# Holding the late attention products behind the FFN products in TensorE's order

## The chip, the core and the metric

The kernel runs on one core of a Trainium2 chip. The metric is the device time of one execution in microseconds (us). TensorE (PE) multiplies, VectorE (DVE), ScalarE (ACT) and GpSimd (POOL) do the elementwise work, and SyncE (SP) issues nearly all the transfers. Each engine works through its own queue in order.

## The reference

A windowed attention is followed by an FFN whose activation is a rational function. Of 768 keys a query keeps the first 8 and the 96 up to its own.

```python
scores = scale * np.matmul(q, k.transpose(0, 1, 3, 2)) + bias      # 4 batches, 8 heads, 768 rows, 64 wide
a = softmax(np.where(keep, scores, -1e9))
x = np.matmul(a, v).transpose(0, 2, 1, 3).reshape(3072, 512)
h = x @ w_in                                                       # 512 -> 2048
P = a0 + a1*h + a2*h*h + a3*h*h*h
Q = 1 + |b0|*|h| + |b1|*h*h
out = (P / (Q + 1e-6)) @ w_out                                     # 2048 -> 512
```

## The kernel before

**Units.** The attention is cut into 96 units: a unit u is 128 query rows and two heads. Eight units make a chunk of 256 rows. The FFN is cut into 96 steps f, eight per chunk: step f makes 256 of the 2048 hidden columns for the chunk's 256 rows. So step f of chunk c can begin only when all eight units of the chunk have delivered their rows of x, and chunk c is units 8c to 8c+7 and FFN steps 8c to 8c+7.

**FFN step.** `st_ffn1` (line 280) makes the FFN's first products, 24 of 256 columns into a PSUM tile `h` (two buffers). `st_ew1` to `st_ew4` evaluate the rational function: lines 304 to 306 on ACT, 311 and 312 on DVE, 313 on POOL, 320 and 321 on ACT, 325 to 327 on DVE, 335 on ACT and 336 on POOL, which end in the tile `g`. `st_ffn2` (line 356) makes the second products, 12 of 512 columns into `acc`, two steps after the first products.

**Late attention.** Units from 24 (`PLAIN`) on take a longer way. `st_split` splits k and q into two parts (line 418 ACT, 419 POOL) and sends the q part through two DMAs (lines 422, 423, tile `qT`). `st_score` makes four products (line 442, tile `s`) and the masked result (line 455, DVE); `st_soft` the exponential (line 465, ACT). `st_turn` transposes blocks on DVE (lines 538, 540) and writes them to DRAM (line 542, tile `put`); `st_back` reads them back (line 550, tile `pT`). Every four units `st_pv` makes the products of V and P (line 577, tile `o`; `o24` is units 24 to 27), and `st_x` scales them (line 603, DVE) and stores x as a high and a low part (`xh`, line 608, ACT; `xl`, line 609, DVE).

**What sets the order.** The loop over t in `windowed` emits the steps. Each call of `on` sets a priority for what it emits, from the step's number times 1000 and a table `PRI`. A scheduler then lays out every engine's queue: of what it believes ready it takes the smallest priority. It has no instruction to keep attention and FFN in step with each other. In the loop, f trails t by 10 to 14 steps.

Of the kernel before, what the change touches and what calls it, by code (L numbers as in the profile page):

```python
# [35 lines left out]
PLAIN = 24  # L36
# [73 lines left out]
def tile_kernel(ctx: ExitStack, tc: tile.TileContext, q, k, qk, v, n_global, n_local,  # L110
                w_in, w_out, ca, cb, out):
    nc = tc.nc
# [26 lines left out]
    def st_load(u, other=nc.sync):  # L139
        c, t, p, b, i = unit(u)  # L140
        hs = slice(2 * p, 2 * p + 4)
        r = slice(i * P, (i + 1) * P)
        if u >= PLAIN:
            nat[u // 2] = pl.ldp.tile([P, 2, 2, P], F32, tag="nat", name=f"kq{u}")
            nc.sync.dma_start(out=nat[u // 2], in_=qk[b, i, p // 2])
            return
        n = pl.ldp.tile([P, 2, 4, D], F32, tag="nat", name=f"nat{u}")
        nc.sync.dma_start(out=n[:, 0], in_=q[b, hs, r, :].rearrange("h s d -> s h d"))
        other.dma_start(out=n[:, 1], in_=k[b, hs, r, :].rearrange("h s d -> s h d"))
        nat[u // 2] = n  # L150
# [73 lines left out]
    def pieces(kind, n):  # L224
        if kind:
            return [(1, 2 * (n % 2) + x, n // 2) for x in range(2)]
        return [(0, 2 * n + x) for x in range(2)]
# [60 lines left out]
    def is_last(f):  # L288
        return f == NU - 1 and not pl.split
# [325 lines left out]
    def windowed(lates):  # L615
        first = [key for t in sorted(WSCHED) for kind, j in WSCHED[t] for key in pieces(kind, j)][0:GBUFS + 3]
        scope = ExitStack()
        pl.early = scope.enter_context(tc.tile_pool(name="early", bufs=1))
        pl.rr = const.tile([P, Q], F32, name="rr")
        pl.rT = const.tile([P, Q], F32, name="rT")  # L620
        nc.gpsimd.memset(pl.rr, 1.0)
        pl.kF = pl.early.tile([P, NPAIR, 2, P], F32, name="kF")
        pl.kGF = pl.early.tile([P, NPAIR, G], F32, name="kGF")
        pl.qz = pl.early.tile([P, 3, 2, P], F32, name="qz")
        nc.scalar.dma_start(out=ni[:, 0:2], in_=n_local.bitcast(I32).partition_broadcast(1))
        nc.scalar.dma_start(out=ni[:, 2:4], in_=n_global.bitcast(I32).partition_broadcast(1))
        st_load(0, nc.scalar)
        st_load(2, nc.scalar)
        st_load_v(0)
        st_load_v(2)  # L630
        nc.scalar.preload_act_table_set("natural_log_exp_and_others")
        for n, key in enumerate(first):
            fetch(key)
        make_identity(nc, ident)
        for x in range(2):
            nc.gpsimd.memset(pl.qz[(1 - x) * D:(2 - x) * D, :, x, :], 0.0)
        one = tmp("one")[0:1, 0, 0:P]
        n1 = pl.early.tile([1, 4], F32, name="n1")
        nc.gpsimd.memset(one, 1.0)
        nc.vector.tensor_copy(out=n1, in_=ni)  # L640
        n_ps = pl.ps_r.tile(sh, F32, tag="r", name="n_ps")
        nc.tensor.matmul(out=n_ps[:, 0, 0:4], lhsT=one, rhs=n1, start=True, stop=True)
        nc.vector.tensor_copy(out=nf, in_=n_ps[:, 0, 0:4])
        nl, ng = nf[:, 0:1], nf[:, 2:3]
        scr = tmp("scr").rearrange("p a (b w) -> p (a b) w", w=P)
        scr = [scr[:, x, :] for x in range(4)]
        window_masks(nc, scr, masks[:, 2, 2, :], masks[:, 2], nl, ng)
        load_coef()

        base = tc.cur_priority  # L650

        def scaled_mask(h):
            if 0 <= h < H and h != 2:
                nc.vector.tensor_scalar(out=masks[:, h], in0=masks[:, 2], scalar1=2.0 ** (2 - h), scalar2=None,
                                        op0=ALU.mult)

        def turn(f):
            return f + EARLY_LAG + (LAG - EARLY_LAG) * min(max(f - FPC, 0), 2 * FPC) / (2 * FPC)

        f = -1  # L660
        for t in range(NU + LAG + F2 + 1):
            step = int(turn(f + 1)) <= t
            f += step
            when = {True: 1000 * turn(f), False: 1000 * t}
            pri = {True: PRI_A if f < FPC else PRI, False: PRI_A if t < FPC + EARLY_LAG else PRI}

            def on(name, fn, u, *args, ffn=False, more=0):
                if 0 <= u < NU:
                    tc.cur_priority = int(base + when[ffn] + pri[ffn][name] + more)
                    fn(u, *args)  # L670

            def ffn(name, fn, u, *args):
                if step:
                    on(name, fn, u, *args, ffn=True)

            def pv(u, more):
                on("pv", st_pv, u, more=more)
                on("x", st_x, u, more=more)

            def behind(n):  # L680
                now, past = t - n, t - n - 1
                return [u for u in ((past,) if past >= PLAIN else ()) + ((now,) if now < PLAIN else ())]

            if t % 2 == 0:
                if t + 4 < PLAIN:
                    on("load", st_load, t + 4)
                if t + 2 >= PLAIN:
                    on("load", st_load, t + 2)
                if t + 4 < PLAIN:
                    on("load", st_load_v, t + 4)  # L690
                elif t - 4 >= PLAIN:
                    on("load", st_load_v, t - 4)
            for u in behind(1):
                on("score", st_score, u)
                on("soft", st_soft, u)
                on("sums", st_sums, u)
            if t == PLAIN:
                scope.close()
                pl.late = lates.enter_context(tc.tile_pool(name="late", bufs=1))
                pl.kq = pl.late.tile([P, 2, 2, 3, 2, P], FR, name="kq")  # L700
                pl.kG = pl.late.tile([P, 2, NPAIR, G], FR, name="kG")
            if t == PLAIN:
                for h in range(H):
                    on("load", scaled_mask, h)
            ffn("ffn1a", st_ffn1, f, 0)
            if t < PLAIN:
                on("qkT", st_qkT, t)
            if t % 2 == 0 and t - 4 >= PLAIN:
                on("turn", st_turn, t - 4)
            if t % 2 == 0 and t - 6 >= PLAIN:  # L710
                on("back", st_back, t - 6, more=65)
            if t % 4 == 2 and t - 6 >= PLAIN:
                on("turn", st_put_rows, t - 6)
            if t % 4 == 0 and t - 8 >= PLAIN:
                on("back", st_get_rows, t - 8)
            if t % 4 == 1 and t - 9 >= PLAIN:
                pv(t - 9, 0)
            if t < PLAIN:
                on("qkE", st_qkE, t)
            elif t % 2 == 0:  # L720
                on("qkE", st_split, t)
            if not is_last(f - 1):
                ffn("ew3", st_ew3, f - 1)
            for u in behind(1):
                on("norm", st_norm, u)
            ffn("ffn1b", st_ffn1, f, 1)
            if is_last(f) and step:
                st_ew4(f - 1)
                last_half(f, 0)
                last_half(f, 1)  # L730
            else:
                ffn("ew1", st_ew1, f)
                if not is_last(f - 1):
                    ffn("ew4", st_ew4, f - 1)
                ffn("ew2", st_ew2, f)
            g = f - F2 if f - F2 < NU - HELD else f - F2 - 1 if f - F2 > NU - HELD else NU
            ffn("ffn2a", st_ffn2, g, 0)
            if t - 2 < PLAIN:
                on("pT", st_pT, t - 2)
            ffn("ffn2b", st_ffn2, g, 1)  # L740
            if t % 2 and t - 3 < PLAIN and spread(t - 3):
                on("turn", st_put_rows, t - 3)
                on("back", st_get_rows, t - 3, more=70)
            if t % 2 and t - 3 < PLAIN:
                pv(t - 3, 0 if t < FPC + EARLY_LAG else 700)
            for n, (kind, j) in enumerate(WSCHED.get(t, ())):
                tc.cur_priority = base + 1000 * t + pri[False]["dec"] + 50 * n
                for key in pieces(kind, j):
                    decode(key)
            if step:  # L750
                for n, key in enumerate(list(full)[SPLITS.get(f - 1, 0):SPLITS.get(f, 0)]):
                    tc.cur_priority = int(base + when[True] + pri[True]["wsplit"] + 4 * n)
                    split_w(key)
        tc.cur_priority = base + 1000 * (NU + LAG + F2 + 5)
# [165 lines left out]
```

## Time and profile before

| | us |
|---|---|
| median of 3 runs (lowest, highest) | 736.69 (736.0, 739.11) |
| the profiled execution: its time | 743.32 |
| the profiled execution: its span, first to last instruction | 741.5 |
| TensorE busy in the span | 707.9 (95%) |
| ACT busy | 569.3 (77%) |
| DVE busy | 537.0 (72%) |
| POOL busy | 426.4 (58%) |

TensorE's matmuls are pipelined, so its busy time does not say that it runs at its peak. How far apart matmuls start says that, and where it sits idle says what it waits for.

### The profile page before, as it was taken

Reading aid. Unit: us, or ns where it says so; the run is one execution under the profiler, and the core shown is the slowest. Engines: PE = TensorE matmul, PEld = TensorE weight load, DVE = VectorE, ACT = ScalarE, POOL = GpSimd, SP = SyncE. Lnnn points to the kernel's source line nnn. Section 1 sums busy time; section 2 is a strip of 40 time slices with the busy share of each in tenths; the row PEclk is TensorE's granted clock in tenths of the full one; section 3 lists DMA queues with packets and bytes.
Section 4 is the critical chain, followed back from the end, with each engine's and each line's share of the span. In section 5 each row is a group of like instructions: output and inputs, shape, how many; then the busy total and the mean of one; then the engine's idle time right before and its main releaser. Section 6 shows DMA issues by size and latency. Waiting matters only on the chain.

```text
span 741.5 us, 13943 instructions
## 1 busy us (share of the span) xinstructions
PE 707.9 (95%) x4618; PEld 601.1 (81%) x4618; DVE 537.0 (72%) x1215; ACT 569.3 (77%) x1232; POOL 426.4 (58%) x421
## 2 busy tenths in 40 slices
PE   5899799999799989999999999999999999999996
PEld 4576367788698778899988888888988889988994
DVE  5777996885877767677877776667786777865665
ACT  6898866888788877688888886667888877866664
POOL 4398775578765664457565764444657646444441
PEclk9999899999899999999999999999999999999999
DMA  9886600114677688016667561010246613510001
GB/s 260 265 247 195 187 23 14 59 47 119 195 211 228 193 219 214 22 37 198 181 186 208 153 191 52 1 35 23 72 143 195 189 47 114 169 50 1 30 0 35
DMA packets 96502, 92.73 MB, mean 125 GB/s; under 512 B 47140, under 2 KB 78500, under 8 KB 96420
## 3 DMA queue, kind: packets, MB, share of 16 engines
q1 hardware_dynamic: 95216, 91.22, 42.3%
q8 instruction: 39, 0.64, 0.4%
q10 hardware_dynamic: 1204, 0.52, 0.3%
q14 instruction: 43, 0.35, 0.1%
HBM read 58.59 MB, written 23.68 MB: 111 GB/s over the span
## 4 chain that ended last, share of the span: by engine, by line
PE 83%; DMA 5%; ACT 4%; DVE 3%; POOL 2%; SPq 1%; issue 1%; POOLq 0%; DVEq 0%; ACTq 0%
PE h L280 32%; PE acc L356 31%; PE o L577 6%; PE s L442 4%; PE acc L351 4%; PE h L272 3%; PE s L436 2%; POOL kq L419 1%; DMA put<-tb 1%; DMA pT<-put 1%; DMA r<-in_moe_w_in_dram 1%; PE tp L526 1%; ACT pr L465 1%; DMA r<-in_moe_w_out_dram 1%; DVE pr L455 1%
## 5 line engine op out<-in xcount | busy, mean ns | idle before, releaser
L313 POOL TENSOR_TENSOR fa<-fa,fs 128x512 f32<-128x512 f32 x95 | 122.8, 1293 | 153.0 <-ACT fs L306 142.0
L280 PE MATMUL h<-xh,win_l 128*128 128x256 f32 x704 | 199.1, 283 | 0.0
L356 PE MATMUL acc<-wout_l,g 128*128 128x512 f32 x352 | 139.4, 396 | 0.0
L280 PEld LDWEIGHTS h<-xh,win_l 128*128 128x128 f32 x704 | 133.5, 190 | 2.5
L336 POOL TENSOR_TENSOR g<-fu,g 128x512 fp32r<-128x512 f32 x87 | 112.3, 1291 | 38.3 <-ACT g L335 32.0
L304 ACT ACTIVATE fu<-h,coef 128x512 f32<-128x512 f32 (+1 forms) x97 | 74.7, 771 | 60.5 <-PE h L280 55.8
L325 DVE SCALAR_TENSOR_TENSOR fu<-fu,coef,q 128x512 f32<-128x512 f32 (+1 forms) x97 | 71.5, 737 | 64.6 <-ACT q L321 63.6
L419 POOL TENSOR_TENSOR kq<-kq,kq 64x512 fp32r<-64x512 f32 x72 | 93.3, 1295 | 32.2 <-ACT kq L418 22.1
L465 ACT ACTIVATE pr<-pr,stats 128x256 f32<-128x256 f32 (+1 forms) x192 | 92.6, 485 | 5.5 <-DVE stats L455 4.9
L320 ACT ACTIVATE fs<-fa,coef 128x512 f32<-128x512 f32 (+1 forms) x97 | 69.7, 719 | 34.1 <-POOL fa L313 32.7
L311 DVE TENSOR_TENSOR fu<-fu,h 128x512 f32<-128x512 f32 (+1 forms) x97 | 65.5, 675 | 40.6 <-ACT fs L306 36.5
L356 PEld LDWEIGHTS acc<-wout_l,g 128*128 128x128 f32 x352 | 66.5, 189 | 11.5
L312 DVE SCALAR_TENSOR_TENSOR fu<-fu,coef,h 128x512 f32<-128x512 f32 (+1 forms) x97 | 70.9, 730 | 1.8
L326 DVE SCALAR_TENSOR_TENSOR q<-fa,coef,q 128x512 f32<-128x512 f32 (+1 forms) x97 | 72.1, 743 | 0.0
L306 ACT ACTIVATE fs<-h,coef 128x512 f32<-128x512 f32 (+1 forms) x97 | 65.9, 679 | 3.5 <-DMA out_dram<-o 1.6
L305 ACT ACTIVATE fa<-h,coef 128x512 f32<-128x512 f32 (+1 forms) x97 | 65.4, 675 | 3.3 <-DVE q L326 3.2
L327 DVE SCALAR_TENSOR_TENSOR fu<-q,fu 128x512 f32<-128x512 f32 (+1 forms) x97 | 65.9, 679 | 1.4
L577 PE MATMUL o<-pT,vt 128*64 128x128 f32 x704 | 59.9, 286 | 6.6 <-DMA pT<-put 5.5
L577 PEld LDWEIGHTS o<-pT,vt 128*64 128x64 f32 x704 | 41.3, 138 | 23.7 <-issue 15.6
L538 DVE STREAM_TRANSPOSE tb<-pr 128x512 f32<-128x512 f32 x60 | 42.0, 704 | 24.8 <-DMA put<-tb 21.0
L321 ACT ACTIVATE q<-fs 128x512 f32<-128x512 f32 (+1 forms) x97 | 57.8, 596 | 1.7
L335 ACT CAST g<-fu 128x512 fp32r<-128x512 f32 (+1 forms) x89 | 54.7, 615 | 5.6 <-DVE fu L327 5.2
(260 smaller groups left out, 1895.8 us busy)
## 6 DMA issues: line engine op xcount, KB each, us to landing
put<-tb SPq DMA_DIRECT2D x30, 512.0 KB
pT<-put SPq DMA_DIRECT2D x120, 128.0 KB
kq<-in_qk_dram SPq DMA_DIRECT2D x36, 256.0 KB
qT<-kq SPq DMA_DIRECT2D x72, 128.0 KB
r<-in_moe_w_in_dram SPq DMA_DIRECT2D x16, 512.0 KB
r<-in_moe_w_out_dram SPq DMA_DIRECT2D x16, 512.0 KB
vt<-in_v_dram SPq DMA_DIRECT2D x48, 128.0 KB
out_dram<-o SPq DMA_DIRECT2D x23, 256.0 KB
```

Of the source, the lines that this page charges most:

```text
L280: nc.tensor.matmul(out=hps[f][:, y, :], lhsT=w[:, fs], rhs=x[:, ct, :], start=(n == 0), stop=(n == 3 * NCT - 1))
L304: nc.scalar.activation(out=u, in_=h, func=AF.Identity, scale=a3, bias=a2)
L312: nc.vector.scalar_tensor_tensor(out=u, in0=u, scalar=a1, in1=h, op0=ALU.add, op1=ALU.mult)
L313: side(f).tensor_tensor(out=a, in0=a, in1=s, op=ALU.add)
L320: nc.scalar.activation(out=s, in_=a, func=AF.Ln, bias=q1)
L325: nc.vector.scalar_tensor_tensor(out=u, in0=u, scalar=a0, in1=r, op0=ALU.add, op1=ALU.mult)
L326: nc.vector.scalar_tensor_tensor(out=r, in0=a, scalar=q1, in1=r, op0=ALU.add, op1=ALU.mult)
L336: side(f).tensor_tensor(out=g[:, 1, ys], in0=u, in1=g[:, 0, ys], op=ALU.subtract)
L356: nc.tensor.matmul(out=acc, lhsT=gs[f][:, z, y, ts], rhs=w, start=(ft == 0 and n == 0), stop=(ft == NFT - 1 and n == 2))
L419: nc.gpsimd.tensor_tensor(out=at[other], in0=raw[own], in1=at[own], op=ALU.subtract)
L465: nc.scalar.activation(out=d, in_=d, func=AF.Exp, scale=-1.0, bias=st[:, x:x + 1], accum_out=st[:, 2 + 2 * x:3 + 2 * x])
L577: nc.tensor.matmul(out=o_ps[x * D:(x + 1) * D, y, :], lhsT=vt[:, 2 * (y % 2) + x, :], rhs=turned_p(u0 + y, x, w), start=(n == 0), stop=(n ...
```

## The change

For each loop step t the change notes in `ended[t]` the last TensorE instruction of the FFN's first products (`ffn1b`). From unit 24 on the first score product of a unit gets an order dependency on `ended[t - 1]`, and the first product of a V and P run one on `ended[t]`. Both sides are on TensorE, so that no semaphore and no instruction is added: the dependency binds the scheduler alone.

```diff
         base = tc.cur_priority
+        here = nc.cur_bb.bb
+        ended = {}
+
+        def products(n):
+            return [x for x in list(here.instructions)[n:] if x.engine == mybir.EngineType.PE]
+
+        def behind_ffn(t, n):
+            own = products(n)
+            if own and t in ended:
+                tc.add_manual_dep(own[0], ended[t].name, mybir.DependencyInfo(
+                    mybir.DependencyClass.NoSync, mybir.DependencyReason.DATA), reason="order of late steps")
...
             def pv(u, more):
+                n = len(here.instructions)
                 on("pv", st_pv, u, more=more)
+                if u >= PLAIN:
+                    behind_ffn(t, n)
                 on("x", st_x, u, more=more)
...
             for u in behind(1):
+                n = len(here.instructions)
                 on("score", st_score, u)
+                if u >= PLAIN:
+                    behind_ffn(t - 1, n)
                 on("soft", st_soft, u)
...
+            n = len(here.instructions)
             ffn("ffn1b", st_ffn1, f, 1)
+            ended[t] = (products(n) or [ended.get(t - 1)])[-1]
+            if ended[t] is None:
+                del ended[t]
```

**TensorE's queue where the late units begin.** The number behind `s`, `h` and `o` is the unit, the FFN step and the first unit of a run; `g13` is the g of FFN step 13. Before:

```order
L442 MATMUL s26_2008<-kq_1743 128x256
...
L280 MATMUL h16_2018<-xh2_1380,w1_0_0h_1114 128x256
...
L442 MATMUL s27_2085<-kq_1743 128x256
...
L442 MATMUL s28_2163<-kq_1743 128x256
L280 MATMUL h16_2018<-xl2_1381,w1_2_0h_1036 128x256
...
L442 MATMUL s29_2253<-kq_1743 128x256
...
L442 MATMUL s30_2323<-kq_1743 128x256
L356 MATMUL acc1_0_1458<-w0_10h_1828,g13_1871 128x512
...
L442 MATMUL s31_2354<-kq_1743 128x256
L442 MATMUL s30_2323<-kq_1743,qT30_2206 128x256
...
L577 MATMUL o24_2381<-pT24_2192,vt24_2006 64x128 x4
```

The same place in the queue of the change:

```order
L442 MATMUL s26_2008<-kq_1743 128x256
...
L280 MATMUL h16_2018<-xh2_1380,w1_0_0h_1114 128x256
...
L442 MATMUL s27_2085<-kq_1743 128x256
...
L356 MATMUL acc1_0_1458<-w0_10h_1828,g13_1871 128x512
...
L280 MATMUL h17_2098<-xh2_1380,w1_0_0h_1114 128x256
...
L442 MATMUL s28_2163<-kq_1743 128x256
...
L280 MATMUL h18_2174<-xh2_1380,w1_0_1h_1196 128x256
...
L442 MATMUL s29_2253<-kq_1743 128x256
...
L280 MATMUL h19_2264<-xh2_1380,w1_0_1h_1196 128x256
...
L442 MATMUL s30_2323<-kq_1743 128x256
```

Six units' scores stood within one FFN step, with the first products of V and P right behind; now one unit stands behind each FFN step, and all 24 first products of step 16 stand together.

**TensorE's queue where a chunk's last run of V and P ends.** `o36` is the last run of the chunk whose FFN begins with `h32`. In the change:

```order
L577 MATMUL o36_3342<-pT36_3101,vt36_2886 64x128
...
L280 MATMUL h31_3329<-xh3_2390,w1_0_3h_1718 128x256
...
L356 MATMUL acc3_0_2961<-w0_10h_1828,g29_3297 128x512
...
L442 MATMUL s44_3410<-kq_1743 128x256
...
L356 MATMUL acc3_0_2961<-w0_10h_1828,g29_3297 128x512
...
L280 MATMUL h32_3420<-xh4_3021,w1_0_0h_1114 128x256
```

Before, the same run ended eight FFN steps earlier:

```order
L577 MATMUL o36_3342<-pT36_3101,vt32_2597 64x128
...
L442 MATMUL s44_3410<-kq_1743 128x256
...
L442 MATMUL s45_3497<-kq_1743 128x256
...
L280 MATMUL h24_2735<-xh3_2390,w1_0_0h_1114 128x256
```

The run o36 moved from ahead of FFN step 24 to ahead of the last half of step 31, one step ahead of the one that needs it.

**DVE's queue at that place.** In the change:

```order
L326 SCALAR_TENSOR_TENSOR q30_3364<-fa30_3289,coef_63,q30_3364 128x512
L603 TENSOR_TENSOR o36_3342<-o36_3342,wbyf_2344 128x512
L327 SCALAR_TENSOR_TENSOR fu30_3288<-q30_3364,fu30_3288 128x512
L455 ISA pr44_3415,stats_64<-s44_3410,masks_66 128x256
...
L609 TENSOR_TENSOR xl4_3022<-o36_3342,xh4_3021 128x4x128
```

Two operations of other work now stand between the scaling of o36 and the low part of x, and the scaling stands behind the function's steps of FFN step 30.

## Rows read from the trace of the kernel before

**Rows 1.** Stretches: length; busy PE, PEld, DVE, ACT, POOL; clock, DMA share, GB/s
```profile
150.00:200.00 50.00, 45.53 (x318) 39.56 (x318) 36.41 (x98) 42.25 (x99) 39.60 (x39) 0.99 0.39 107
200.00:250.00 50.00, 48.54 (x344) 42.56 (x341) 38.82 (x101) 41.96 (x96) 30.52 (x36) 0.94 0.75 217
250.00:300.00 50.00, 46.68 (x335) 39.85 (x334) 34.64 (x88) 36.92 (x84) 28.60 (x26) 1.00 0.78 209
350.00:400.00 50.00, 50.00 (x380) 44.84 (x379) 37.99 (x93) 43.02 (x96) 31.48 (x34) 1.00 0.65 192
```
**Rows 2.** Waits of TensorE from 165 us on; us in total, times, longest us
```profile
PE o L577 <- DMA pT<-put: 5.5, 2, 2.8
PE s L442 <- DMA qT<-kq: 1.5, 2, 1.0
PE h L280 <- DVE fu L312: 1.0, 1, 1.0
PE acc L356 <- POOL g L336: 0.6, 1, 0.6
```
**Rows 3.** TensorE in time, first long wait: start, us, instruction, [idle <-releaser]
```profile
180.27 0.28 PE L442 MATMUL s<-kq 128*128 128x256 f32 x1
...
181.22 0.39 PE L280 MATMUL h<-xl,w_0h 128*128 128x256 f32 x1 [0.19 <-DVE xl L609]
...
196.55 0.28 PE L442 MATMUL s<-kq 128*128 128x256 f32 x1
199.48 1.12 PE L577 MATMUL o<-pT,vt 128*64 128x128 f32 x8 [2.65 <-DMA pT<-put]
...
202.40 0.63 PE L356 MATMUL acc<-wout_l,g 128*128 128x512 f32 x1
202.83 0.63 PE L356 MATMUL acc<-w_14h,g 128*128 128x512 f32 x1
```
**Rows 4.** The chain that ended last, near that wait; start us, us, what
```profile
187.85 3.07 DMA put<-tb
...
195.96 3.38 DMA pT<-put
```
**Rows 5.** Stretches of 5 us, columns as in rows 1
```profile
200.00:205.00 5.00, 5.00 (x23) 4.28 (x20) 4.13 (x14) 3.14 (x6) 2.85 (x5) 0.50 0.88 265
...
270.00:275.00 5.00, 3.32 (x22) 2.55 (x23) 2.14 (x5) 4.00 (x13) 4.06 (x4) 1.00 0.94 245
```
**Rows 6.** TensorE in order of time, around a piece of a V and P run
```profile
158.83 0.39 PE L356 MATMUL acc<-w_5h,g 128*128 128x512 f32 x1
159.15 0.66 PE L577 MATMUL o<-pT,vt 128*64 128x128 f32 x8
159.74 0.38 PE L280 MATMUL h<-xh,w_2h 128*128 128x256 f32 x1
159.96 0.28 PE L280 MATMUL h<-xl,w_2h 128*128 128x256 f32 x1
```
**Rows 7.** The chain that ended last: long pieces of V and P, and the last chunk's start
```profile
355.99 1.90 PE o L577 x32
...
678.03 1.46 PE o L577 x24
679.49 1.62 PE h L280 x12
681.11 2.79 PE acc L356 x12
683.89 2.84 PE h L280 x24
```
**Rows 8.** Lines 603, 608, 609: ns min/median/max, first and last start us
```profile
L603 DVE TENSOR_TENSOR o<-o,wbyf x18: 667/698/700, 200.6 to 679.5; 128x512 f32<-128x512 f32 x18
L608 ACT CAST xh<-o x26: 357/585/615, 56.5 to 680.3; 128x512 fp32r<-128x512 f32 x18, 128x256 fp32r<-128x256 f32 x8
L609 DVE TENSOR_TENSOR xl<-o,xh x26: 409/683/692, 56.9 to 680.9; 128x512 fp32r<-128x512 f32 x18, 128x256 fp32r<-128x256 f32 x8
```

## The prediction

> **What bounds the kernel now.** I read the busy time by stretches first. From 350 to 400 us TensorE is busy for all of 50.00 us at full clock; from 150 to 300 us it is not: 45.53, 48.54 and 46.68 us of 50, with a mean clock of 0.94 in the middle stretch [rows 1]. Busy TensorE here means one that starts a matmul as soon as it can. 24 first products of 256 columns take 2.84 us, 0.12 each; 12 second products of 512 columns 2.79 us, 0.23 each [rows 7]. So where TensorE is full, time goes by the count of matmuls, which the change leaves as it is. What can be won is idle time, lost clock, and what it costs to switch between kinds of matmul.
>
> The list of waits says who makes TensorE idle after 165 us: the read-back of the turned P (5.5 us in two waits), qT (1.5), a first product that waits for DVE to free its PSUM buffer (1.0) and a g that is late on POOL (0.6), 8.6 us in all [rows 2]. The matmuls in order of time show how the first of them arises. The score of unit 27 starts at 180.27. Its P is transposed, written out (187.85, 3.07 us) and read back (195.96, 3.38 us) [rows 4], and the run of V and P over units 24 to 27 goes on at 199.48, after 2.65 us of idleness [rows 3]. That way takes 19.2 us. In TensorE's order of before only some 13 us of work stand between that score and that part of the run; scores of units 28 to 33 are among it, which nothing needs yet. TensorE is in order, so the late read-back also holds the FFN products behind it, and they were ready. The chain through the DMAs is the limit of this stage, because the attention was pulled ahead of the FFN work that could have covered it.
>
> **The change, part by part.** It removes and adds no instruction. From unit 24 on it puts one unit's scores behind each FFN step and the runs of V and P one FFN step ahead of where they are needed.
>
> *The waits.* From the score of unit 27 to the run o24 the new order has 72 first products, 16 score products and 48 second products: 88 x 0.12 + 48 x 0.23 = 21.6 us, against the 19.2 us that the data took. That 19.2 us was measured with DVE and POOL crowded by six units at once, so I expect the data earlier. For the other 17 runs the same count gives 20 to 31 us from the last score to the run; before it was 14 us at the second run. Splitting q and k moves too, on ACT, POOL and SP. In the new order each split stands two FFN steps ahead of its score, some 10 us ahead of need once the 3 to 4 us of its transfer are taken off. SP's queue has the write, the four read-backs, two qT transfers and two loads for each pair of units as before, now at an even pace. I therefore take all 8.6 us out. Bounds: 0 if every wait comes back elsewhere, 8.6 if none does; I take the upper one, because from 350 to 400 us the same transfers run at a DMA share of 0.65 without idling TensorE [rows 1].
>
> *The clock.* Behind the 2.65 us wait the clock is at its lower level, 1.2 GHz (0.50), for the whole stretch from 200 to 205 us [rows 5], and second products follow one another by 0.43 us [rows 3] instead of 0.23. At 0.43 instead of 0.23, 5 us of work could have been done in 2.7: 2.3 us that go with the wait. Bounds 0 to 2.3; I take 2.3. The second wait of about that length ends at 271.68, and there the clock stays at 1.00 [rows 5]. The Trainium skill, "TensorE: Matmul & The Clock Gate", section "Loop structure matters more than you think", says that a loop which waits for a DMA ahead of its matmuls drops TensorE to half clock. By that rule both long waits would have cost it, and the sum would be 2.3 us larger; the trace bears it out at one of two, so one is counted.
>
> *The pieces.* A run of V and P that is cut up by other products costs more. Eight records of it start at 159.15, 0.32 after the last second product instead of 0.23; they last until 159.74, which is 0.59; and the first product behind them takes 0.22 until the next, instead of 0.12 [rows 6, 7]. 32 records in one piece take 1.90 us [rows 7], so each further record costs (1.90 - 0.59)/24 = 0.055 us, and a piece by itself 0.09 + (0.59 - 8 x 0.055) + 0.10 = 0.34 us. Counted in the two orders, the 18 runs stand in 52 pieces before and in 38 after: 14 x 0.34 = 4.8 us saved. Bounds: 0, if a switch hides part of another delay that then comes to light, to 6, if pieces of odd length cost more than this one of even length.
>
> *What is late next.* At the start of FFN step 16 its eighth product needs the low part of x, which came at 181.22 in the order of before, after 0.19 us of idleness, with five score products filling the time ahead of it [rows 3]. Now nothing fills it: about 0.6 us more, between 0 and 1. Then there are nine chunk starts (FFN steps 24, 32 and so on to 88). In the new order 4.2 to 4.7 us of TensorE work stand between the last V and P products and the first product that needs them; before it was 32 to 70 us at five of the nine. The way is scaling (0.698, DVE), high part (0.585, ACT), low part (0.683, DVE) [rows 8]: 2.0 us, plus what stands ahead on DVE and between, one to three operations of 0.4 to 0.7 us. That makes 2.7 to 4.1 us, just inside. If DVE is late by one more operation at each, 9 x 0.5 = 4.5 us. The nearest row is the last chunk's start: the run ends at 679.49, step 88 begins at 683.89, 4.40 us later, and TensorE never idled [rows 7]. So I take 1.2 us for the nine, and 0 to 4.5 as bounds.
>
> *What stays covered.* With one unit per FFN step ACT is the next engine in line. In the full stretch it is busy for 43.02 us of 50, DVE for 37.99, POOL for 31.48 [rows 1], and that stretch carried more units than steps, so the even pace asks less of them. If ACT fell behind, first products would wait for their PSUM buffer.
>
> The sum: 8.6 + 2.3 + 4.8 - 0.6 - 1.2 = 13.9 us. The profiled execution took 743.32 us (span 741.5), so it would take 729.4. It lies 6.6 us above the median of 736.69. If all of that excess sat in the waits removed, 7.3 us would be left of the gain; the stages before 150 us move as much data and are as likely a place. I take the gain whole: 736.7 - 13.9 = 722.8, so 723 us.
>
> **Rivals.**
> *The waits are shorter without a profile, or the pieces cost nothing.* Gain 7.3 to 9.1 us, 727.6 to 729.4. [...] Against: a DMA chain of 19 us over 13 us of cover does not vanish by 6 us. Still faster.
> *The waits come back in other places.* The new order was laid out by the same scheduler, which believed that 13 us of cover were enough. If the runs o24 and o28 still wait and each chunk start loses 1 us, that is 5.5 + 2.3 + 9 x 1, against the 13.9 and 1.2 above: about 736 us, no change. Against it are the 21.6 us counted.
> *The chunk starts become the bound.* The even pace takes away the lead of the attention, so any lateness on DVE or ACT at a chunk start stops TensorE, nine times, and could bring the lower clock with it. It decides when a start loses over 13.9/9 = 1.5 us beyond what is counted; it is slower by over 0.5% from 2 us on. At 2.5 us each it gives 736.7 - 13.9 + 22.5 = 745 us. For it: 4.2 us of cover against up to 4.1 us of way. Against: the last chunk's start without a wait.
> That the change does not do what it says is excluded by the order of the queue.
>
> **How the numbers follow.** The forecast has 0.60, the first rival 0.25, no change 0.09, slower 0.06. A measurement of this kernel can tell about 0.5% from no change, 3.7 us: faster means under 733.0, slower over 740.4. So faster 0.85, same 0.09, slower 0.06. The range reaches down to 715, where the pieces give 6 us, the new waits nothing and some idle issue time goes too, and up to 734, which takes in the first rival and the bounds of the new waits.
>
> **What would show it.** In the profile after, no wait of TensorE on pT or qT of over 1 us from 165 us on; clock 1.00 in every stretch from 150 to 700 us; TensorE busy 49 us or more of each 50 from 200 us on; the last run of V and P late as before. Wrong would be waits of first products on lines 608 or 609 at chunk starts, or ACT busy above 47 of 50 us with first products waiting on line 312.

## The result, and the profile after

The changed kernel takes **725.78 us** (median of 4 runs, 723.95 to 728.39); the kernel before took 737.42 in the runs beside it (736.0 to 739.11). The ratio is 0.9844 with an interval of 0.9805 to 0.9883, a gain of 11.6 us. On another chip, later, it took 725.22 (5 runs, 723.78 to 726.11) beside 740.13 of before (17 runs), 0.9798 [0.976, 0.9836], a gain of 14.9. Forecast were 723 us and a gain of 13.9, which lies between the two pairs; but some of its steps were wrong, and their errors cancel in part, as shown below.

The profiled execution took 725.09 us, span 723.3, against 743.32 and 741.5 before. So the profile gained 18.2 us where the medians gained 11.6.

From the head of the page of after, the busy time of TensorE and its count of instructions, and the granted clock in 40 slices (before: 707.9 us with the same 4618 instructions, and 13943 in all; the 85 that are gone are semaphore instructions):

```profile
span 723.3 us, 13858 instructions
PE 697.9 (96%) x4618; PEld 597.9 (83%) x4618; DVE 539.3 (75%) x1215; ACT 569.8 (79%) x1232; POOL 427.9 (59%) x421
PEclk9999999999999999999999999999999999999998
```

The same count of matmuls took 10.0 us less busy time. That is no faster arithmetic: a matmul at the lower clock, or at a switch between kinds, counts as longer. The 8.6 us of waits that went (below) come on top, and the two together are about the 18.2 of the span.

The same stretches of 50 us as in [rows 1], of after:

```profile
150.00:200.00 50.00, 49.64 (x346) 44.02 (x345) 39.11 (x93) 42.29 (x95) 38.31 (x36) 1.00 0.32 88
200.00:250.00 50.00, 50.00 (x345) 44.37 (x344) 38.41 (x87) 42.18 (x89) 31.23 (x33) 1.00 0.57 174
250.00:300.00 50.00, 49.62 (x352) 43.39 (x352) 37.90 (x86) 40.20 (x86) 28.76 (x27) 1.00 0.47 140
350.00:400.00 50.00, 50.00 (x346) 44.29 (x345) 39.06 (x87) 42.54 (x90) 32.16 (x31) 1.00 0.45 139
```

The three stretches that were short of work are full to within 0.4 us, and the clock is 1.00 in each. The DMA share between 200 and 300 us fell from 0.75 and 0.78 to 0.57 and 0.47: part of the transfers that six units at once had crowded there now come later (the share between 300 and 350 us went from 0.25 to 0.49).

All waits of TensorE from 165 us on, of after (columns as in [rows 2]):

```profile
PE acc L356 <- POOL g L336: 0.4, 2, 0.2
PE h L280 <- DVE fu L312: 0.2, 1, 0.2
```

No wait on pT or qT is left: 0.6 us in all, where before had 9.2 with the entries too small for [rows 2].

The chain that ended last, of after, at the run o24 and at the last chunk's start (start us, us, engine, what it makes, line, count):

```profile
204.22 0.80 PE o L577 x10
205.02 1.12 PE acc L356 x4
206.14 0.37 PE o L577 x4
206.51 0.43 PE h L280 x2
...
230.77 1.90 PE o L577 x32
...
658.72 1.89 PE o L577 x30
660.61 1.62 PE h L280 x12
662.23 2.78 PE acc L356 x12
665.02 2.84 PE h L280 x24
```

The run that had waited 2.65 us for its pT [rows 3] now starts at 204.22 without a wait. It is still cut into pieces by second products. At the last chunk's start 4.41 us stand between the run and the step that needs it (660.61 to 665.02; 4.40 before, [rows 7]), again without a wait.

The comparisons below go by the late stage of each profiled execution: its span less the time at which the first score of the late units starts, so that what happened ahead of the change's reach stays out. That start varies from 168.4 to 172.2 us between executions. The rows are of before and of after:

```profile
L442 PE MATMUL s<-kq x144: 274/283/415, 172.2 to 642.2; 128*128 128x256 f32 x144
```

```profile
L442 PE MATMUL s<-kq x144: 274/281/387, 171.0 to 628.9; 128*128 128x256 f32 x144
```

The late stage took 741.5 - 172.2 = 569.3 us before and 723.3 - 171.0 = 552.3 after: 17.0 us less.

### The profile page after: what moved, and what is told of

It reads as the page before. It is cut to its first block, busy times and chain, and to the rows that moved or that the text cites. A ratio compares the mean times of both kernels' runs of the same rounds, so it can differ in the third digit from the quotient of the medians.

```text
span 723.3 us, 13858 instructions
## 1 busy us (share of the span) xinstructions
PE 697.9 (96%) x4618; PEld 597.9 (83%) x4618; DVE 539.3 (75%) x1215; ACT 569.8 (79%) x1232; POOL 427.9 (59%) x421
## 4 chain that ended last, share of the span: by engine, by line
PE 88%; ACT 5%; DMA 3%; DVE 2%; issue 1%; SPq 0%; POOL 0%; ACTq 0%; DVEq 0%
PE h L280 34%; PE acc L356 33%; PE o L577 6%; PE s L442 4%; PE acc L351 4%; PE h L272 3%; PE s L436 2%; ACT pr L465 1%; DMA r<-in_moe_w_in_dram 1%; PE tp L526 1%; DMA out_dram<-o 1%; PE tk L390 1%; DMA nat<-in_q_dram 1%; DMA r<-in_moe_w_out_dram 0%; ACT kq L418 0%
## 5 line engine op out<-in xcount | busy, mean ns | idle before, releaser
L455 DVE CUSTOM_DVE_ANT_0 pr<-s,masks 128x256 f32<-128x256 f32 (+1 forms) x128 | 45.2, 386 | 30.6 <-PE s L442 21.1
L577 PE MATMUL o<-pT,vt 128*64 128x128 f32 x704 | 55.2, 283 | 0.3 <-DVE stats L455 0.3
```

What stands on the lines that cost most here:

```text
L577: nc.tensor.matmul(out=o_ps[x * D:(x + 1) * D, y, :], lhsT=vt[:, 2 * (y % 2) + x, :], rhs=turned_p(u0 + y, x, w), start=(n == 0), stop=(n ...
```

## What the change really does

Half of it does nothing. The diff asks for `ended[t]` when it places a run of V and P of step t, but `pv(t - 9, 0)` is called in the loop ahead of `ffn1b`, which sets `ended[t]`. The entry is not there yet, and `behind_ffn` returns without a word. With that half taken out of the source, TensorE's queue is the same, instruction by instruction. The last V and P products of o36 show it too: in the order of the change, printed ahead of the prediction, they stand in the middle of the 24 first products of step 31, not behind them. The only effective edit is the hold on the scores; the runs came later by themselves, because their scores did. My prediction took both dependencies as real. In the experiments, "held" for a run of V and P means that it really is.

## Experiments

Two sets, each with its own runs of before beside it. In the first (both half holds, the runs behind all first products, and the same cut in four) before took 738.43 us (17 runs, 733.32 to 741.23); in the second 740.13 (17 runs, 736.74 to 745.46). "Pieces" are uninterrupted groups of V and P products in TensorE's queue, counted run by run over the 18 runs from unit 24 on. "Waits" are those from 165 us on.

| kernel | median us (runs) | ratio to before | late stage us | waits of TensorE us | pieces |
|---|---|---|---|---|---|
| before | 738.43, 740.13 | 1 | 569.3 | 9.2 | 52 |
| change, repeat | 725.22 (5) | 0.9798 [0.976, 0.9836] | 552.7 | 0.9 | 38 |
| scores held below unit 44 only | 746.59 (6) | 1.0109 [1.0087, 1.0131] | 575.7 | 12.9 | 55 |
| scores held from unit 44 only | 730.13 (6) | 0.9881 [0.9856, 0.9905] | 557.6 | 5.7 | 38 |
| runs behind all first products | 732.12 (6) | 0.9918 [0.989, 0.9947] | 558.9 | 10.1 | 24 |
| the same, each run cut in four | 735.78 (12) | 0.996 [0.994, 0.998] | 562.5 | 0.2 | 75 |
| runs behind half the first products | 719.3 (5) | 0.9725 [0.9686, 0.9763] | 547.7 | 1.1 | 25 |
| runs behind second products | 741.72 (12) | 1.0026 [1.0003, 1.0049] | 569.3 | 19.0 | 18 |
| runs behind half, scores free | 730.83 (6) | 0.9889 [0.9852, 0.9925] | 558.0 | 9.3 | 30 |

**The scores held only at the start.**

```diff
-                if u >= PLAIN:
+                if PLAIN <= u < 44:
                     behind_ffn(t - 1, n)
```

> Scores are held for units 24 to 43 alone; from unit 44 on the scheduler is free as before. V and P runs stand in 55 pieces from unit 24 on (52 before, 38 after). Waits theory with pieces at 0.34 us each: no wait on pT or qT between 165 and 300 us, about 726 + 17 x 0.34 = 732 us. If pieces cost nothing and the waits are all of the gain: 726. If the waits were an artefact of the profiled execution: about 737.

Measured: 746.59 us, slower than before by 1.1%, and none of the three times that were expected. Its waits of TensorE from 165 us on, the five largest entries:

```profile
PE o L577 <- DMA pT<-put: 4.6, 3, 2.4
PE o L577 <- DMA qT<-kq: 2.4, 1, 2.4
PE o L577 <- DVE stats L455: 2.1, 1, 2.1
PE o L577 <- DMA put<-tb: 1.5, 1, 1.5
PE s L442 <- DVE stats L455: 1.1, 1, 1.1
```

The first stage is mended (50.00 of 50 us at clock 1.00 from 200 to 250), and what it had been spared came back where units 44 and up may run ahead. TensorE in order of time there, columns as in [rows 3]:

```profile
345.30 0.28 PE L442 MATMUL s<-kq,qT 128*128 128x256 f32 x1
347.72 1.09 PE L577 MATMUL o<-pT,vt 128*64 128x128 f32 x16 [2.14 <-DVE stats L455]
...
351.75 0.28 PE L442 MATMUL s<-kq 128*128 128x256 f32 x1
354.47 1.09 PE L577 MATMUL o<-pT,vt 128*64 128x128 f32 x16 [2.44 <-DMA pT<-put]
```

DVE at the first of the two waits:

```profile
347.57 0.09 DVE L455 DVE_READ_ACCUMULATOR2_ANT stats<- 128x1 f32 x1
```

The second is the pattern of [rows 3]: scores in a burst, and a run close behind them that waits for its pT. The first has the same burst but another cause: `s` and `o` share three PSUM buffers (tag `t`), and the run starts when DVE has read the last score. So it is the burst that makes the wait, wherever it is allowed, and not something particular to the place where the late units begin. Against the change the late stage is 23.4 us longer: 12.3 us of waits (12.9 - 0.6), 17 more pieces at 0.29 to 0.40 each (priced below), 4.9 to 6.8, and about 3.5 of clock (mean 0.93 over 600 to 650 us), 20.7 to 22.6 in all.

**The scores held only later.** The complement: `if u >= 44:` in the same place.

> Scores are held from unit 44 on alone; units 24 to 43 run ahead as before. 38 pieces. Waits theory with pieces: the waits on pT and qT and the lower clock behind them stay in the profile, 14 pieces fewer save 4.8 us: about 732.5 us. If pieces cost nothing: 737. If the gain of the change came from the even pace of the rest: 726.

Measured: 730.13 us, between the 726 and the 732.5 that were expected for an even pace and for the waits. It keeps 2.9 us of waits on pT in two places and 2.8 in others, and its clock is 0.72 from 195 to 200 us. With the same 38 pieces as the change its late stage is 5.3 us longer, near the 5.1 us of additional waits and some 1.7 of clock. So the waits and the clock that are left in the first stage are worth about 5 us of the 17.0. The rest is the 14 pieces (4.1 to 5.6 us) and waits that this half of the hold takes away too, above all the one of 2.85 us that ended at 271.68 before.

**The runs really held.** The call is moved behind the line that sets `ended[t]`, so that the second half of the diff takes effect:

```diff
-            if t % 4 == 1 and t - 9 >= PLAIN:
-                pv(t - 9, 0)
...
             ended[t] = (products(n) or [ended.get(t - 1)])[-1]
             if ended[t] is None:
                 del ended[t]
+            if t % 4 == 1 and t - 9 >= PLAIN:
+                pv(t - 9, 0)
```

> The V and P runs are emitted behind the first products of their step, so that their order dependency takes effect: 24 pieces instead of 38. Pieces at 0.34 us: 14 x 0.34 = 4.8 us below the change, about 721 us. If pieces cost nothing: 726. Chunk starts as the bound: a start has about 6 us of other work ahead, so no more waits than in the change; if they show, 728 or more.

Measured: 732.12 us, where 721 was expected, or 726 if pieces cost nothing, or 728 and more if the chunk starts became the bound. The waits that came are others. The change as its words describe it would have been worse than what it is. Its waits of TensorE from 165 us on:

```profile
PE acc L356 <- ACT g L335: 5.7, 3, 2.2
PE h L280 <- DVE fu L312: 2.5, 3, 1.7
PE acc L356 <- POOL g L336: 1.4, 1, 1.4
PE h L280 <- DVE xl L609: 0.5, 1, 0.5
```

Not pT but g is late: the second products of the step ahead, which need what ACT and POOL make of its first products. The five largest waits lie at 379.93, 425.17, 480.08, 534.38 and 589.51 us, about one per chunk; four are for g, the one at 534.38 for a PSUM buffer of `h` (line 312). A run of 1.90 us that stood among first products had been cover for that way; behind them it isn't. With 14 pieces fewer (4.1 to 5.6 us) the late stage is still 6.6 us longer: 9.5 of waits and 1.7 of clock outweigh them.

**The same, cut in four.** Each run is emitted there too, but its four parts are tied behind first products 3, 6, 9 and 12 of the second half step in turn (`halves[t]` are the products of `ffn1b`):

```diff
-                if u >= PLAIN:
-                    behind_ffn(t, n)
+                own = products(n)
+                if u >= PLAIN and len(halves[t]) == 12:
+                    k = len(own) // 4
+                    for y in range(4):
+                        to = halves[t][3 * y + 2]
+                        for x in own[y * k:(y + 1) * k]:
...
```

> As pv_behind, but each run is cut into four parts with three first products between them: 75 pieces instead of 24, the last part at the same place. Pieces at 0.34 us: 51 x 0.34 = 17 us above pv_behind, about 738 us. If pieces cost nothing: as pv_behind. Waits on the data should not differ from pv_behind.

Measured: 735.78 us, 3.7 above the kernel with whole runs there instead of the 17 expected, and the waits, which were expected to stay, differ. Its waits of TensorE from 165 us on, and the row that gives the first late score:

```profile
PE h L280 <- DVE fu L312: 0.2, 1, 0.2
```

```profile
L442 PE MATMUL s<-kq x144: 274/281/387, 171.8 to 639.4; 128*128 128x256 f32 x144
```

Two readings. Spread among the first products the runs cover g again: the 10.1 us of waits are gone. And with no waits and no lower clock in the late stage, the 10.2 us by which it (734.3 - 171.8 = 562.5) is longer than the change's 552.3, with the 0.4 us by which its waits are shorter, belong, as far as is known, to its 37 additional pieces: **0.29 us for each**.

**The change again, beside the second set.**

> The change itself beside the next three on the same chip: ratio to before 0.984, about 726 us, no wait over 0.5 us from 165 us on, 38 pieces.

Measured: 725.22 us; late stage 552.7, waits 0.9 us. The profile repeats, and so does the median; what differs between the pairs is before, 737.42 and 740.13.

**The runs held behind half of the first products.** Scores as in the change; a run gets its dependency on the last product of `ffn1a` of its step, which stands in the loop ahead of the call, so that it exists:

```diff
+        half = {}
...
-        def behind_ffn(t, n):
+        def behind_ffn(t, n, ended=ended):
...
-                    behind_ffn(t, n)
+                    behind_ffn(t, n, half)
...
+            n = len(here.instructions)
             ffn("ffn1a", st_ffn1, f, 0)
+            half[t] = (products(n) or [None])[-1]
```

> Scores held as in the change; in addition each V and P run is held behind the first half of the first products of its own step (a dependency that takes effect). The order is that of the change but for 25 pieces instead of 38, and every run ends where it ended. Pieces at 0.3 us: 13 x 0.3 = 3.9 us below the change. If the small pieces cover waits on g: waits on g and on line 312 appear and the time is that of the change or above.

Measured: **719.3 us** (717.75 to 720.71), ratio 0.9725: 5.9 us faster than the change (3.9 were expected) and the fastest kernel of this study. Its waits of TensorE from 165 us on, and its first late score:

```profile
PE acc L356 <- POOL g L336: 0.7, 2, 0.6
PE h L280 <- DVE fu L312: 0.4, 1, 0.4
```

```profile
L442 PE MATMUL s<-kq x144: 274/281/387, 168.4 to 622.5; 128*128 128x256 f32 x144
```

The late stage is 716.1 - 168.4 = 547.7 us, 5.0 less than in the repeat of the change, with 0.2 us more of waits and 13 pieces fewer: 5.2/13 = **0.40 us for each**. The 12 first products of the second half step stay behind the run and still cover g.

**The runs held behind the second products.** The run is emitted behind `ffn2b` of its step and tied to its last product; scores stay tied to the first products:

```diff
-            if t % 4 == 1 and t - 9 >= PLAIN:
-                pv(t - 9, 0)
...
+            first[t] = ended.get(t)
...
+            ended[t] = (products(n) or [ended.get(t)])[-1]
...
+            if t % 4 == 1 and t - 9 >= PLAIN:
+                pv(t - 9, 0)
```

> Scores held as in the change; V and P runs held behind the second products of their step: 18 whole pieces, and one step of second products less ahead of a chunk start, about 3.3 us of other work instead of 4.2 to 4.7. Pieces: 20 x 0.3 = 6 us below the change, were that all. Chunk starts as the bound: a way of 2.7 to 4.1 us against 3.3 gives up to 0.8 us at nine starts, waits on lines 608 and 609. Waits on g, as where the runs were emitted behind the first products: 5 to 10 us more, 730 or above.

Measured: 741.72 us (730 or above was expected), the whole gain gone, although every run is in one piece (18). Its waits of TensorE from 165 us on:

```profile
PE acc L356 <- ACT g L335: 9.4, 8, 1.5
PE h L280 <- DVE fu L312: 5.1, 6, 1.0
PE acc L356 <- POOL g L336: 4.5, 14, 0.5
```

One place of the pattern, TensorE and then ACT in order of time:

```profile
423.24 0.28 PE L280 MATMUL h<-xh,win_l 128*128 128x256 f32 x1
424.70 0.50 PE L356 MATMUL acc<-w_0h,g 128*128 128x512 f32 x1 [1.18 <-ACT g L335]
...
429.12 0.36 PE L280 MATMUL h<-xh,w_2h 128*128 128x256 f32 x1 [0.87 <-DVE fu L312]
```

```profile
420.47 1.26 ACT L418 CAST kq<-kq 64x512 fp32r<-64x512 f32 x2 [0.19 <-PE s L442]
421.76 0.59 ACT L364 COPY o<-acc 128x512 f32<-128x512 f32 x1
...
424.04 0.60 ACT L335 CAST g<-fu 128x512 fp32r<-128x512 f32 x1
```

At a chunk's first FFN step ACT has the copies of the last chunk's output (line 364), a split of q and k (line 418) and the exponentials in its queue ahead of the cast that makes g, which starts at 424.04; TensorE, in order, has nothing else to do there. These waits come back every 56 us or so (the first at 255.85, 313.01 and 368.64). No wait on lines 608 or 609 shows, although only about 3.3 us of products now stand between the last V and P product of a chunk and the first product that needs it. Against the change the late stage is 17.0 us longer: 18.4 of waits, less 20 pieces at 0.29 to 0.40, 5.8 to 8.0, makes 10.4 to 12.6. The other 4.4 to 6.6 us are in the trace too. A wait costs more than its idle time: the first products stand 0.12 us apart but each record lasts 0.28, so that idleness is counted only from the end of the record. From 423.24 to 424.70 are 1.46 us, 1.34 more than between two first products, and the row has 1.18. Each of the 28 waits here hides some 0.16 us in this way, and so do the 3 in the change: 25 more, 4.0 us. And the clock is 0.88 and 0.78 in the two stretches of 5 us from 480 us on, behind a wait of 1.52 us that ended at 481.83: 1.7 us.

```profile
485.00:490.00 5.00, 5.00 (x29) 4.58 (x28) 3.82 (x7) 3.42 (x6) 2.62 (x3) 0.78 0.05 13
```

**The runs held, the scores free.** As the kernel of 719.3 us, but with the two lines that hold the scores taken out.

> Scores are free as before, only the V and P runs are held, behind the first half of their step's first products. The distance from the last score to its run grows as in the change; 30 pieces. If the cover between score and run is the cause: no wait on pT, 22 pieces fewer than before, about 726 to 728 us, with up to 2 us of waits on qT in the first burst. If the bursts of scores themselves are the cause, by crowding DVE, ACT and POOL: waits on g and line 312 and 733 us or more.

Measured: 730.83 us, between the 726 to 728 and the 733 or more that were expected of the two causes. Its waits from 165 us on, the four largest:

```profile
PE acc L356 <- POOL g L336: 3.8, 3, 1.6
PE acc L356 <- ACT g L335: 2.4, 1, 2.4
PE acc L356 <- ACT o L364: 1.6, 2, 0.8
PE s L442 <- DMA qT<-kq: 1.0, 1, 1.0
```

The waits on pT are gone with the scores still in bursts: it is work between score and run that removes them, and holding the run gives it as well as holding the scores. But the total is 9.3 us, what it was before, and now it is g that is late. At the wait that ends at 196.55 the exponentials of a burst stand in ACT's queue ahead of the cast that makes g; at the one that ends at 309.40 it is a split of q and k on POOL (line 419, 2.65 us for two). The 11.3 us of late stage gained over before go with 22 fewer pieces (6.4 to 8.8 us) and the clock (2.3 to 3.4). So the even pace of the scores has a worth of its own: with it, 719.3; without, 730.83, of which 5 pieces more (30 against 25) are 1.5 to 2.0 us.

## Why the prediction was right, and where not

The signs that the prediction named came out: clock 1.00 in every stretch from 150 to 700 us, TensorE busy for over 49 us of each 50 from 200 us on, ACT for at most 42.88, and no wait on lines 608 or 609.

*The waits, 8.6 us.* Right, in size and cause: [rows 2] has become 0.6 us, and nothing came back elsewhere. In the trace of after the score of unit 27 starts at 181.43 and the run at 204.22: 22.8 us, where 21.6 were counted and the data of before had needed 19.2. That the DMA chain is to blame only where a burst stands ahead of it is shown by the two partial holds. With the 0.16 us that each wait hides, five waits fewer are worth 0.8 us more than the rows say.

*The clock, 2.3 us.* Right in kind, and too small: it was worked out from one stretch of 5 us, but the ones beside it were low too. Of before:

```profile
195.00:200.00 5.00, 2.35 (x15) 1.79 (x15) 4.15 (x9) 4.34 (x11) 3.30 (x3) 0.90 0.88 257
205.00:210.00 5.00, 5.00 (x35) 4.51 (x36) 3.12 (x6) 3.59 (x12) 1.46 (x2) 0.92 0.47 148
```

With the 0.50 between them that is 3.4 us at most, 0.5 of it ahead of 200 us, where TensorE waited for part of the time. In the change all three are at 1.00. The rule of the Trainium skill that the prediction set beside this term ("TensorE: Matmul & The Clock Gate", section "Loop structure matters more than you think") is given there for a loop with a far longer wait ahead of every matmul. That section does not say what a single wait of 2.65 or 2.85 us does, so this case neither bears it out nor speaks against it.

*The pieces, 14 x 0.34 = 4.8 us.* Right: the experiments give 0.29 and 0.40 for one, 4.1 to 5.6 us for 14. The step rested on a single row of eight records [rows 6] and could have been far off; two kernels with 37 more and 13 fewer pieces bracket it, if nothing but the pieces makes the difference that their waits and clock leave.

*New waits, 0.6 at step 16 and 1.2 at the chunk starts.* Wrong, both on the careful side. No wait on line 609 above 0.3 us is in the trace of after, and the last chunk's start has its 4.41 us without one. With these two terms at nothing the sum is 8.6 + 2.3 + 4.8 = 15.7, against 17.0 of late stage in the profile; what the waits hide and the rest of the lower clock make up for that. (The way at a chunk start adds up to 2.4 to 4.1 us from its own terms, not 2.7 to 4.1.)

*The gain of the profile taken whole to the median.* This is the step that failed, and it hid the one above. The profile, forecast at 729.4, took 725.09 and gained 18.2 us; the medians gained 11.6 in the first pair, 14.9 in the second. The profiled execution of before lay 6.6 us above the median of 736.69; that of after lies at its median (725.09 and 725.78). That a sum too small for the profile came out near the medians is luck. What the excess was is not shown, but it goes with the clock: in the second set the runs of before with a mean granted clock of 0.990 or less took 739.18 to 745.46 us, those with 0.994 or more 736.74 to 737.32 (0.989 in the profiled one). The mean clocks of the two groups are 0.988 and 0.995, and 0.007 of 740 us is 5 us; their mean times are 4.9 us apart. The first rival put the excess down to the waits themselves. Its 7.3 to 9.1 us lie below both pairs, and the kernel that was held only at the start, with 8.5 us of waits on DMAs, scatters over 745.05 to 748.94 alone. Where in those runs the lower clock lay was not measured.

*The run bound to `ended[t]`, and "That the change does not do what it says is excluded by the order of the queue."* Wrong. I read in the queue that the runs had come later and took the dependency for the cause. The order that spoke against it was printed beside the diff: o36 amid the first products of step 31. The number was not hurt, since terms came from the real queue.

*The chunk starts as the bound.* Not borne out, neither here nor with only 3.3 us of cover. Lateness of ACT and DVE does stop TensorE about once per chunk when runs stand too late, but at g (lines 335 and 336), a wait that none of the rivals named.

*Waits that come back in other places.* Not in the change; but it is what half a hold does, at 746.59 us. (Its price in the prediction was off by 2 us: 5.5 + 2.3 + 9 against 13.9 + 1.2 is 1.7 us above 736.7, 738.4 and not 736.)

## What to carry to other kernels

Where an in-order engine waits for a chain through other engines and DMAs, count the work that stands between the chain's start and its end in the queue, and hold the start of work that nobody needs yet with dependencies of order alone; hold it everywhere, since a partial hold moved the stall to where running ahead begins. A block that is moved out of the way was also cover for something: here runs behind half of the first products gained 5.9 us, behind all of them lost some 6, behind the second products some 16. And a dependency on an instruction that is emitted later may silently not exist: compare the queue with and without each part of an edit before believing what it says.

## What the runs showed of the hardware

The length of a wait does not tell whether the lower clock (1.2 GHz) follows. After 2.65 us the clock was 0.50 for 5 us, after the next one that ended at 271.68 it stayed at 1.00 [rows 5]. The kernel with runs behind all first products has both again (columns as in [rows 1]), a wait of 2.18 us at 425.17 and one of 1.87 at 589.51:

```profile
425.00:430.00 5.00, 4.83 (x32) 4.43 (x33) 4.08 (x7) 3.04 (x6) 3.46 (x3) 1.00 0.56 165
...
590.00:595.00 5.00, 5.00 (x28) 4.82 (x27) 4.39 (x7) 2.41 (x4) 3.35 (x3) 0.66 0.62 173
```

The longer wait cost no clock, the shorter one a third of 5 us. In the kernel held only at the start, 2.39 us at 601.22 was followed by 0.75, 2.44 us at 354.47 by 1.00; with the runs behind the second products, 1.52 us at 481.83 by 0.78, 1.50 us at 313.01 by 1.00. What tells them apart no run here shows.

The other surprise is how near to each other the prices of a piece come out: 0.34 us from one place in the trace of before, 0.40 over 13 pieces and 0.29 over 37, for going over to V and P products and back. That is the time of two and a half to three and a half first products.
